# Three more units by rows, later output projections and earlier weight loads in an attention and gMLP kernel

## The chip, the cores and the metric

One core of one Trainium2 chip runs the whole program. The metric is the device time of one execution in microseconds (us), median of several runs. A ratio below is the mean time of one kernel's fast runs over the mean of the other's fast runs of the same rounds, so it is not quite the ratio of the medians quoted beside it. "Faster" or "slower" needs 2%. A *span* is the length of the one profiled execution, from its first to its last instruction, without the start and end of the launch.

## The reference, cut to what matters

```python
# S = 2048, D = 512, 32 query heads, 8 kv heads, Dh = 128, F/2 = 896
mod = (silu(c) @ w_mod).reshape(1, 6, 1, 512)
sa, ca, ga, sb, cb, gb = mod[:, 0], ..., mod[:, 5]
h = layernorm(x) * (1 + ca) + sa
q = (h @ wq) per head;  p = softmax(q @ k.T * Dh ** -0.5);  o = p @ v
x = x + ga * (o @ wo)
h = layernorm(x) * (1 + cb) + sb
z = gelu(h @ w_in);  z1, z2 = z[:896], layernorm(z[896:])
g = w_sp @ z2 + b_sp                      # spatial mixing, 2048 x 2048
out = x + gb * ((z1 * g) @ w_out)
```

## The kernel before

The attention is cut into NU = 128 *units*: 8 groups (one kv head with its 4 query heads) times 16 tiles of 128 queries (NT = 16; a *block* is CT = 4 tiles). *Iteration* u issues the scores of unit u in eight slots. In each slot TensorE also gets a share of an older unit's PV product and, mostly, one *extra*: a matmul of an output projection (`wo`) or of a query projection. A slot without an extra is *bare*. The *excess* of an iteration is its length less the sum of its matmuls at the pitches that the prediction measures.

An ordinary unit computes its scores transposed, so that ScalarE's exponentials can go straight into PV, one iteration later, as 64 matmuls of 129 columns. A unit *by rows* computes them untransposed; the exponentials are summed as they are made, VectorE normalises them, four DMA transposes of 512 KB turn them, and PV follows three iterations later as 16 matmuls of 512 columns.

Names in the profile lines: `hT` is the transposed layer norm, `oT` the transposed output of PV, `z` the hidden tile of the gMLP. The memory of a unit by rows is reused, so its rows stand there as `win_sb`, `wmod_a` or `pn`, and their transpose as `pT` or `wsp`.

```python
TURN_A, TURN_B = 2 * CT, NU - CT - 2          # units by rows: 8, 10, ... 120

def by_rows(u):
    return TURN_A <= u < TURN_B and u % 2 == 0
def pv_at(u):
    return u + 3 if by_rows(u) else u + 1
def wo_at(u):
    return pv_at(u) + (3 if TURN_A <= u < TURN_B else 2)
...
def turn_rows(u, hh):                          # VectorE, then a DMA transpose
    ...
    nc.vector.tensor_scalar(out=rows, in0=rows, scalar1=rinv, scalar2=None, op0=ALU.mult)
    nc.sync.dma_start_transpose(out=pTs[u][:, :, hh * P : (hh + 1) * P], in_=rows)
...
def mod_rows():                                # the rows ga and gb, on all partitions
    ...
    for i, (part, rows) in enumerate(((2, ga_rows), (5, gb_rows))):
        cols = slice(part * NDT, (part + 1) * NDT)
        nc.vector.tensor_copy(out=modc[:, cols], in_=mc_ps[:, i * NDT : (i + 1) * NDT])
        line = dram.tile([D], FP32, name=f"mod{part}")
        nc.gpsimd.dma_start(out=line[:].rearrange("(dt p) -> p dt", p=P), in_=modc[:, cols])
        nc.gpsimd.dma_start(out=rows[:], in_=line[:].partition_broadcast(P))
...
ln1_at(3, (5, 1), (5, 5), (7, 4))              # last layer-norm chunk: statistics, norm, turn
at(NU - CT - 1, 2, lambda: nc.gpsimd.dma_start(out=win_sb, in_=win_dram))
at(4, 4, mod_cols_b)
at(5, 4, mod_rows)

def set_fill(b):                               # query projection of block b as extras
    hole = TURN_A + 1 if (TURN_A + 1) // CT == b - 1 else None
    ...
    for k, fn in enumerate(fs):
        ...
        elif b == 2:
            it, slot = (5, k // 2) if k < 8 else (it, slot)
...
for g in range(1, HKV):                        # weights of group g
    it = (g - 1) * NT
    at(it + 9, 5, lambda g=g: load_k(g))
    at(*((5, 2) if g == 1 else (it + 7, 4)), lambda g=g: load_wq(g, nc.gpsimd))
    at(*((5, 2) if g == 1 else (it + 11, 4)), lambda g=g: load_v(g))
    at(*((5, 2) if g == 1 else (it + 13, 4)), lambda g=g: load_wo(g, nc.gpsimd))
```

`at(iteration, slot, f)` puts f's instructions at that place of every engine's order.

Of the kernel before, what the change touches and what calls it, by code (L numbers as in the profile page):

```python
# [11 lines left out]
FP32 = mybir.dt.float32  # L12
# [3 lines left out]
P = 128  # L16
# [559 lines left out]
def kernel(  # L576
# [19 lines left out]
    nc = tc.nc  # L596
# [3 lines left out]
    REP = HQ // HKV  # L600
# [9 lines left out]
    CT = 512 // P  # L610
# [17 lines left out]
    win_dram = B_w_in.rearrange("(dt p) f -> p dt f", p=P)  # L628
# [11 lines left out]
    stat = fast.enter_context(tc.tile_pool(name="stat", bufs=2))  # L640
# [10 lines left out]
    rall = res.tile([P, NT * HQ], FP32, name="rall")  # L651
# [5 lines left out]
    win_sb = win_t[:].rearrange("p (k f) -> p k f", k=NDT)  # L657
# [61 lines left out]
    def load_wq(g, engine):  # L719
        wqs[g] = early.tile([P, NDT, REP * DH], BF16, name="wq_g")  # L720
        engine.dma_start(
            out=wqs[g][:], in_=wq_dram[:, :, g * REP * DH : (g + 1) * REP * DH]
        )

    def load_v(g):
        v1 = late.tile([P, NKT, DV], BF16, name="v1")
        nc.gpsimd.memset(v1[:, :, DH:DV], 1.0)
        if g > 0:
            nc.gpsimd.dma_start(out=v1[:, :, 0:DH], in_=v_dram[:, g])
        else:  # L730
            nc.sync.dma_start(out=v1[:, 0 : NKT // 2, 0:DH], in_=v_rows)
            nc.sync.dma_start(
                out=v1[:, NKT // 2 : NKT, 0:DH], in_=v_dram[:, 0, NKT // 2 : NKT]
            )
        groups.setdefault(g, {})["v1"] = v1

    def load_wo(g, engine):
        wo_g = late.tile([P, REP, D], BF16, name="wo_g")
        engine.dma_start(out=wo_g[:], in_=wo_dram[:, g * REP : (g + 1) * REP, :])
        groups[g]["wo"] = wo_g  # L740

    def load_k(g):
        kT = early.tile([P, SK], BF16, name="kT")
        nc.sync.dma_start_transpose(out=kT[:], in_=A_k_cache[0, g])
        groups.setdefault(g, {})["kT"] = kT
# [154 lines left out]
    for k in range(2):  # L900
        for dt in (2 * k, 2 * k + 1):
# [3 lines left out]
            else:  # L905
                nc.scalar.activation(
                    out=dst,
                    in_=src,
# [17 lines left out]
    for hf, copy in enumerate((nc.vector.tensor_copy, nc.scalar.copy)):  # L926
        copy(
            out=qTs[0][:, 2 * hf : 2 * hf + 2, 0:P],
            in_=q_ps[hf][:, 0 : 2 * P].rearrange("p (h q) -> p h q", h=2),
# [3 lines left out]
    def qproj(b, heads, c0, n, banks=("misc", "misc")):  # L933

        g, ch = divmod(b, NCH)
        if b not in qTs:
            qTs[b] = early.tile([P, REP, 512], BF16, name="qT")
        one = n * len(heads) <= 512
        ps = {}

        def mm(hh, dt):
            if dt == 0 and (not one or hh == heads[0]):
                ps[0] = bank(banks[hh % 2])
            o0 = (hh - heads[0]) * n if one else 0
            nc.tensor.matmul(  # L945
                ps[0][:, o0 : o0 + n],
                lhsT=wqs[g][:, dt, hh * DH : (hh + 1) * DH],
                rhs=hTs[ch][:, dt, c0 : c0 + n],
                start=(dt == 0),
                stop=(dt == NDT - 1),  # L950
            )
            if dt == NDT - 1 and (not one or hh == heads[-1]):
                hs = heads if one else [hh]
                dst = qTs[b][:, hs[0] : hs[-1] + 1, c0 : c0 + n]
                src = ps[0][:, 0 : len(hs) * n].rearrange("p (h q) -> p h q", q=n)
                nc.vector.tensor_copy(out=dst, in_=src)  # L956

        return [lambda hh=hh, dt=dt: mm(hh, dt) for hh in heads for dt in range(NDT)]
# [4 lines left out]
    NU = HKV * NT  # L963


    TURN_A, TURN_B = 2 * CT, NU - CT - 2

    def by_rows(u):
        return TURN_A <= u < TURN_B and u % 2 == 0

    def pv_at(u):
        return u + 3 if by_rows(u) else u + 1

    def wo_at(u):
        return pv_at(u) + (3 if TURN_A <= u < TURN_B else 2)


    users, homes = dict(pT0=-2, pT1=-1, wsp=CT + 2), {}
# [8 lines left out]
    def at(it, slot, fn):  # L987
        later.setdefault((it, slot), []).append(fn)
# [198 lines left out]
    def load_wsp(tile_, t, st):  # L1187
        nc.sync.dma_start_transpose(
            out=tile_[:, st, :],
            in_=B_w_sp[t * 512 : (t + 1) * 512, st * P : (st + 1) * P],  # L1190
        )
# [35 lines left out]
    ln1_at(2, (2, 4), (3, 1), (4, 5))  # L1227
    ln1_at(3, (5, 1), (5, 5), (7, 4))
    at(2, 5, lambda: nc.gpsimd.dma_start(out=wmod_b, in_=wmod_dram[:, :, 2 * D : NMOD]))
    at(NU - CT - 1, 2, lambda: nc.gpsimd.dma_start(out=win_sb, in_=win_dram))  # L1230
    at(4, 4, mod_cols_b)
    at(5, 4, mod_rows)

    def set_fill(b):


        hole = TURN_A + 1 if (TURN_A + 1) // CT == b - 1 else None
        fs = qproj(b, list(range(REP)), 0, 512, ("misc", "o_ps" if hole else "misc"))
        for k, fn in enumerate(fs):
            it, slot = (b - 1) * CT + k // NDT, k % NDT  # L1240
            if hole:
                it, slot = divmod(hole * NSLOT + k // 2 - 1, NSLOT)
            if b == 1:
                it, slot = 2 + (10 + k) // 16, (5 + k // 2) % 8
            elif b == 2:
                it, slot = (5, k // 2) if k < 8 else (it, slot)
            fill.setdefault((it, slot), []).append(fn)

    def wsp0():
# [2 lines left out]
    at(NU + 1, 0, wsp0)  # L1252
    for st in range(NT):
        at(NU + 1 + st // 4, 2 * (st % 4), lambda st=st: load_wsp(wsp[0], 0, st))
    for g in range(1, HKV):
        it = (g - 1) * NT
        at(it + 9, 5, lambda g=g: load_k(g))
        at(*((5, 2) if g == 1 else (it + 7, 4)), lambda g=g: load_wq(g, nc.gpsimd))
        at(*((5, 2) if g == 1 else (it + 11, 4)), lambda g=g: load_v(g))
        at(*((5, 2) if g == 1 else (it + 13, 4)), lambda g=g: load_wo(g, nc.gpsimd))  # L1260


    zs = {}
# [90 lines left out]
    for it in range(NU + 6):  # L1354
        if it < NU:
            if it % CT == 0 and it // CT + 1 < NB:
                set_fill(it // CT + 1)
        elif it == NU:
            free_a.close()
            z2p = fast.enter_context(tc.tile_pool(name="z2p", bufs=1))  # L1360
            zs["z2"] = z2p.tile([P, NT, FH], BF16, name="z2")
        pvs = [u for u in (it - 5, it - 3, it - 1) if 0 <= u < NU and pv_at(u) == it]
        wos = [u for u in range(max(it - 6, 0), min(it - 2, NU)) if wo_at(u) == it]
        wf = [fn for u in wos for fn in wo_proj(u)]
        for i in range(NSLOT):
# [37 lines left out]
    for f in range(NFT):  # L1403
# [6 lines left out]
        out=ok1[:], in0=rall[:], scalar1=1.0 / SAFE, scalar2=None, op0=ALU.is_ge  # L1410
# [8 lines left out]
        out=bad[:], in0=okm[:], scalar1=-1.0, scalar2=1.0, op0=ALU.mult, op1=ALU.add  # L1419
# [137 lines left out]
```

## Time and profile before

| | before |
|---|---|
| time, three runs | 1315.22 us (1314.62 to 1316.67) |
| span of the profiled run | 1311.9 us |
| TensorE / ScalarE / VectorE busy | 99% / 85% / 52% |
| granted TensorE clock | 1.000 |
| period of two iterations in the steady part | 17.44 us |

The table says where not to look: the time is TensorE's, and it is a sum of equal periods. Only the head (iterations up to 13), the tail and 0.18 us per unit are left. The lines are in the prediction.

### The profile page before, as it was taken

How to read it: one execution, taken by the hardware profiler on the slowest of the kernel's cores; microseconds unless marked ns; L12 is line 12 of the kernel's file. 1: busy time of each engine (PE TensorE's matmuls, PEld its weight loads, DVE VectorE, ACT ScalarE, POOL GpSimd, SP SyncE). 2: the span in 40 equal slices, each digit the busy share in tenths (PEclk: the TensorE clock that was granted, in tenths of full speed). 3: DMA queues.
4: the chain of work that ended last, by engine and by line, in shares of the span. 5: the costliest groups of instructions: out<-in, count | busy, mean ns of one | idle time of the engine just before them, and what ended most of it. 6: DMA issues, size and time to landing. Idle time of an engine off the chain costs nothing.

```text
span 1311.9 us, 24470 instructions
## 1 busy us (share of the span) xinstructions
PE 1304.1 (99%) x9623; PEld 741.0 (56%) x9623; DVE 682.6 (52%) x1675; ACT 1111.1 (85%) x1517; POOL 54.0 (4%) x96
## 2 busy tenths in 40 slices
PE   9999999999999999999999999999999999999998
PEld 5665555555555555555555555555555556644445
DVE  5644544444445454444545444444454577884444
ACT  7899999999999999999999999999999998650000
POOL 1200000000000000000000000000000011120000
PEclk9999999999999999999999999999999999999999
DMA  7589778977787797779986798678866673254300
GB/s 181 119 118 178 130 140 147 148 130 149 153 156 142 140 140 142 142 139 136 160 162 121 144 142 156 124 150 153 153 125 128 116 131 85 58 138 100 73 20 27
DMA packets 592170, 170.51 MB, mean 130 GB/s; under 512 B 581712, under 2 KB 588112, under 8 KB 592048
## 3 DMA queue, kind: packets, MB, share of 16 engines
q1 hardware_dynamic: 585024, 149.74, 64.5%
q0 software_dynamic: 4432, 16.91, 5.1%
q10 hardware_dynamic: 2592, 2.23, 0.5%
q8 instruction: 77, 1.26, 0.4%
q14 instruction: 45, 0.37, 0.1%
HBM read 21.89 MB, written 2.10 MB: 18 GB/s over the span
## 4 chain that ended last, share of the span: by engine, by line
PE 98%; DMA 1%; DVE 0%; ACT 0%; SPq 0%; issue 0%; DVEq 0%
PE o_ps L1080 19%; PE s_ps L1024 18%; PE s_ps L1005 15%; PE o_ps L1059 15%; PE misc L1112 8%; PE misc L945 8%; PE misc L1437 7%; PE s_ps L1271 2%; PE s_ps L1310 2%; PE o_ps L1458 1%; DMA oT<-onorm 1%; PE o_ps L786 1%; PE s_ps L1458 1%; PE misc L855 0%; PE o_ps L945 0%; DVE hT L814 0%
## 5 line engine op out<-in xcount | busy, mean ns | idle before, releaser
L1031 ACT ACTIVATE pT<-s_ps 128x1024 bf16<-128x1024 f32 x560 | 568.5, 1024 | 34.4 <-PE s_ps L1024 11.3
L1080 PEld LDWEIGHTS <-pT 128*128 128x128 bf16 x4480 | 299.6, 98 | 130.8
L1080 PE MATMUL o_ps<-v,pT 128*128 128x129 bf16 x4480 | 344.6, 220 | 0.0
L1024 PE MATMUL s_ps<-qT,kT 128*128 128x512 bf16 x1136 | 337.6, 379 | 0.3 <-ACT pT L1031 0.2
L1005 PE MATMUL s_ps<-kT,qT 128*128 128x512 bf16 x912 | 271.2, 379 | 0.0
L1012 ACT ACTIVATE win_sb<-s_ps 128x1024 bf16<-128x1024 f32 x228 | 233.3, 1024 | 3.4
L1112 PE MATMUL misc<-wo_g,oT 128*128 128x512 bf16 x512 | 194.1, 379 | 0.7 <-DMA oT<-onorm 0.7
L945 PE MATMUL misc<-hT,wq_g 128*128 128x512 bf16 (+2 forms) x520 | 187.0, 371 | 0.1
L1024 PEld LDWEIGHTS <-kT 128*128 128x128 bf16 x1136 | 110.2, 98 | 114.6 <-issue 2.4
L1012 ACT ACTIVATE pn<-s_ps 128x1024 bf16<-128x1024 f32 x152 | 155.4, 1023 | 2.0 <-ACT wmod_a L1012 0.3
L1059 PEld LDWEIGHTS <-v 128*128 128x128 bf16 x912 | 89.2, 98 | 107.7
L956 DVE CAST qT<-misc 128x512 bf16<-128x512 f32 x125 | 85.6, 684 | 123.1 <-PE misc L945 123.1
L1068 DVE CAST oT<-o_ps 128x512 bf16<-128x512 f32 x57 | 39.4, 691 | 192.3 <-PE o_ps L1059 192.3
L1059 PE MATMUL o_ps<-wsp,v 128*128 128x512 bf16 x464 | 137.3, 379 | 0.0
L1059 PE MATMUL o_ps<-pT,v 128*128 128x512 bf16 x448 | 133.2, 379 | 0.0
L1005 PEld LDWEIGHTS <-qT 128*128 128x128 bf16 x912 | 89.1, 98 | 59.8 <-issue 0.2
L1045 DVE TENSOR_TENSOR tot<-rs 128x1 f32<-128x1 f32 x228 | 35.0, 153 | 127.7 <-ACT win_sb L1012 85.3
L1437 PE MATMUL misc<-wsp,z 128*128 128x512 bf16 (+2 forms) x560 | 100.7, 336 | 0.0
L1050 DVE TENSOR_SCALAR win_sb<-win_sb,rall 128x2048 bf16<-128x2048 bf16 x114 | 85.9, 753 | 4.2 <-DVE rall L1048 0.3
L1437 PEld LDWEIGHTS <-z 128*128 128x128 bf16 x560 | 50.6, 98 | 48.5
L1012 ACT ACTIVATE wmod_a<-s_ps 128x1024 bf16<-128x1024 f32 x76 | 77.8, 1024 | 0.0
L1125 DVE TENSOR_TENSOR xacc<-misc,xacc 128x512 f32<-128x512 f32 x112 | 76.1, 679 | 0.0
(110 smaller groups left out, 831.0 us busy)
## 6 DMA issues: line engine op xcount, KB each, us to landing
wq_g<-in_A_wq_dram POOLq DMA_DIRECT2D x7, 512.0 KB, 6.1
v<-in_A_v_cache_dram POOLq DMA_DIRECT2D x7, 512.0 KB, 6.3
wo_g<-in_A_wo_dram POOLq DMA_DIRECT2D x7, 512.0 KB, 10.6
wsp<-in_w_mod_dram POOLq DMA_DIRECT2D x1, 2048.0 KB, 10.8
out_dram<-yout ACTq DMA_DIRECT2D x16, 128.0 KB, 1.7
win_sb<-in_B_w_in_dram POOLq DMA_DIRECT2D x1, 1792.0 KB, 7.9
x_sb<-in_A_x_dram SPq DMA_DIRECT2D x3, 512.0 KB, 5.9
oT<-onorm SPq DMA_TRANSPOSE x71, 2.8
```

The lines of the kernel that those rows point to most:

```text
L945: nc.tensor.matmul(ps[0][:, o0 : o0 + n], lhsT=wqs[g][:, dt, hh * DH : (hh + 1) * DH], rhs=hTs[ch][:, dt, c0 : c0 + n], start=(dt == 0), s ...
L956: nc.vector.tensor_copy(out=dst, in_=src)
L1005: nc.tensor.matmul(s_ps[:, c * 512 : (c + 1) * 512], lhsT=qTs[b][:, hh, jj * P : (jj + 1) * P], rhs=groups[g]["kT"][:, k0 : k0 + 512], sta ...
L1012: nc.scalar.activation(out=rows_of(u, hh)[:, half * HK : (half + 1) * HK], in_=s_ps[:], func=ACT.Exp, scale=inv_sqrt_dh, accum_out=rsums[u ...
L1024: nc.tensor.matmul(s_ps[:, h * 512 : (h + 1) * 512].rearrange("p (r q) -> p r q", r=REP), lhsT=groups[g]["kT"][:, kt * P : (kt + 1) * P], ...
L1031: nc.scalar.activation(out=pTs[u][:, 2 * i : 2 * i + 2, :], in_=s_ps[:].rearrange("p (k q) -> p k q", k=2), func=ACT.Exp, scale=inv_sqrt_dh,)
L1050: nc.vector.tensor_scalar(out=rows, in0=rows, scalar1=rinv, scalar2=None, op0=ALU.mult)
L1059: nc.tensor.matmul(o_pss[u][:], lhsT=groups[g]["v1"][:, kt, 0:DH], rhs=pTs[u][:, kt, :], start=(kt == 0), stop=(kt == NKT - 1),)
L1080: nc.tensor.matmul(o_ps[:, hh % 2, 0 : DH + 1], lhsT=pTs[u][:, kt, hh * P : (hh + 1) * P], rhs=groups[g]["v1"][:, kt, 0 : DH + 1], start=( ...
L1112: nc.tensor.matmul(X_ps[:], lhsT=oTs[u][:, hh, :], rhs=groups[g]["wo"][:, hh, :], start=(hh == 0), stop=(hh == REP - 1),)
L1125: nc.vector.tensor_tensor(out=xaccs[j][:], in0=X_ps[:], in1=xaccs[j][:], op=ALU.add)
L1437: nc.tensor.matmul(g_ps[:, :n], lhsT=z2[:, st, f * P : (f + 1) * P], rhs=wsp[t][:, st, c0 : c0 + n], start=(st == 0), stop=(st == NT - 1 a ...
```

## The change

Its intent: give the cheaper PV to three more units, and fill or remove the small holes at the two ends of the attention.

```diff
-    TURN_A, TURN_B = 2 * CT, NU - CT - 2
+    TURN_A, TURN_B = CT + 2, NU - 2
...
     def wo_at(u):
-        return pv_at(u) + (3 if TURN_A <= u < TURN_B else 2)
+        return pv_at(u) + (3 if u < TURN_B - CT else 2)
...
-    at(NU - CT - 1, 2, lambda: nc.gpsimd.dma_start(out=win_sb, in_=win_dram))
+    at(NU - 2, 4, lambda: nc.gpsimd.dma_start(out=win_sb, in_=win_dram))
...
-            elif b == 2:
-                it, slot = (5, k // 2) if k < 8 else (it, slot)
...
+    def wait_for(u):
+        seen = stat.tile([P, 1], FP32, name="seen")
+        nc.gpsimd.tensor_copy(out=seen[:], in_=rall[:, u * REP : u * REP + 1])
+
+    at(5, 0, lambda: wait_for(3))
     for g in range(1, HKV):
         it = (g - 1) * NT
         at(it + 9, 5, lambda g=g: load_k(g))
-        at(*((5, 2) if g == 1 else (it + 7, 4)), lambda g=g: load_wq(g, nc.gpsimd))
+        at(*((5, 0) if g == 1 else (it + 7, 4)), lambda g=g: load_wq(g, nc.gpsimd))
         (load_v and load_wo likewise)
```

More of the change, by code (lines that the diff above doesn't have):

```diff
@@ L1257 @@
         at(it + 9, 5, lambda g=g: load_k(g))
-        at(*((5, 2) if g == 1 else (it + 7, 4)), lambda g=g: load_wq(g, nc.gpsimd))
-        at(*((5, 2) if g == 1 else (it + 11, 4)), lambda g=g: load_v(g))
-        at(*((5, 2) if g == 1 else (it + 13, 4)), lambda g=g: load_wo(g, nc.gpsimd))
+        at(*((5, 0) if g == 1 else (it + 7, 4)), lambda g=g: load_wq(g, nc.gpsimd))
+        at(*((5, 0) if g == 1 else (it + 11, 4)), lambda g=g: load_v(g))
+        at(*((5, 0) if g == 1 else (it + 13, 4)), lambda g=g: load_wo(g, nc.gpsimd))
     zs = {}
```

## The prediction

> **What bounds the kernel now.** I read the page's engine line first, then the chain of waits, then TensorE's timeline, and only then the DMA issues.
>
> ```profile
> PE 1304.1 (99%) x9623; PEld 741.0 (56%) x9623; DVE 682.6 (52%) x1675; ACT 1111.1 (85%) x1517; POOL 54.0 (4%) x96
> ...
> PE 98%; DMA 1%; DVE 0%; ACT 0%; SPq 0%; issue 0%; DVEq 0%
> ```
>
> TensorE holds 98% of the chain, and the only other share is one DMA wait of 1%. So nothing large can come from removing waits; a gain must be fewer or shorter TensorE pitches, or the few small holes. Since ends of matmuls are modelled, I take pitches from starts. Call the scores of unit u "iteration u"; it has eight slots, each with two score matmuls, a share of an older unit's PV, and perhaps one "extra" (an output-projection or query-projection matmul). Two neighbouring iterations of the steady part, from TensorE's timeline:
>
> ```profile
> 131.90 0.59 PE L1005 MATMUL s_ps<-kT,qT 128*128 128x512 bf16 x2
> 132.34 0.62 PE L1080 MATMUL o_ps<-v,pT 128*128 128x129 bf16 x8
> 132.79 0.38 PE L945 MATMUL misc<-hT,wq_g 128*128 128x512 bf16 x1
> 133.00 0.59 PE L1005 MATMUL s_ps<-kT,qT 128*128 128x512 bf16 x2
> ...
> 140.71 0.59 PE L1024 MATMUL s_ps<-qT,kT 128*128 128x512 bf16 x2
> 141.14 0.59 PE L1059 MATMUL o_ps<-wsp,v 128*128 128x512 bf16 x2
> 141.57 0.38 PE L945 MATMUL misc<-hT,wq_g 128*128 128x512 bf16 x1
> 141.79 0.59 PE L1024 MATMUL s_ps<-qT,kT 128*128 128x512 bf16 x2
> ...
> 149.34 0.59 PE L1005 MATMUL s_ps<-kT,qT 128*128 128x512 bf16 x2
> ```
>
> The first column is the start. An iteration that holds the PV of an ordinary unit (64 matmuls of 129 columns, L1080) takes 140.71 - 131.90 = 8.81 us; one with the PV of a unit by rows (16 of 512, L1059) 149.34 - 140.71 = 8.63 us. Eight small ones take about 0.454 us (0.0567 each), two wide ones 0.432 (0.216 each). A unit by rows is thus worth only 0.18 us of TensorE.
>
> Then I added, iteration by iteration, the matmuls at those pitches and compared with the distance of starts. From iteration 13 to 123 the difference is 0.01 to 0.02 us: TensorE never waits. It waits only in iterations 7 to 12 (0.90, 0.27, 0.15, 0.53, 0.37, 0.31, sum 2.53 us) and a little in 124 and 126 (0.19). Two kinds of wait:
>
> ```profile
> 79.63 0.39 PE L1112 MATMUL misc<-wo_g,oT 128*128 128x512 bf16 x1 [0.72 <-DMA oT<-onorm]
> ...
> 102.35 0.59 PE L1005 MATMUL s_ps<-kT,qT 128*128 128x512 bf16 x2
> 102.78 0.61 PE L1080 MATMUL o_ps<-v,pT 128*128 128x129 bf16 x8
> 103.35 0.59 PE L1005 MATMUL s_ps<-kT,qT 128*128 128x512 bf16 x2
> ```
>
> The first is an output projection that waits for its transposed input. The second is a slot with no extra: TensorE has 0.43 + 0.45 = 0.89 us of work, but the slot lasts 1.00, because ScalarE's exponential with its accumulator read repeats every 1.0 us in a unit by rows (100.19, 101.18, 102.18 in its timeline) and every 0.92 in an ordinary one. With an extra (1.10 us) TensorE is the slower. So bare slots cost, filled ones don't.
>
> Why the transpose was late stands in Pool's timeline and in the chain in order of time:
>
> ```profile
> 60.01 0.81 POOL L721 DMA_DIRECT2D wq_g<-in_A_wq_dram  x1
> ...
> 62.38 0.76 POOL L739 DMA_DIRECT2D wo_g<-in_A_wo_dram  x1
> ...
> 66.82 12.77 DMA oT<-onorm
> ```
>
> Group 1's three loads (512 KB each) were issued at 60 to 62 us, at the same moment as the four transposes of the last layer-norm chunk (61.0 to 66.7). Together they kept the DMA engines busy until about 76; this oT took 12.8 us where the median is 2.8.
>
> **What the Trainium skill says.** "TensorE: Matmul & The Clock Gate", Wait — 56ns, not 53.3ns?: start to start is N / 2.4 GHz + about 2.5 ns when warm; that gives 56.3 ns for 129 columns and 215.8 for 512. The trace agrees (56.7 and 216). The same page's Back-to-back issue gap says about 131 ns for a sustained stream at N = 512; here the measured 216 decides. "Perfetto Trace Analysis", Identifying the Most-Contended Engine, warns that matmul busy share is a poor measure; I therefore used starts, and they say the same. "DMA: Bandwidth & Descriptors", Issuing engines are not separate DMA queues: DMAs of different engines interleave on the same 16 engines. The 12.8 us landing beside Pool's loads agrees.
>
> **The change, part by part.** The order of instructions of the changed kernel, which I read slot by slot, has 144 matmuls fewer: 3 units x (64 - 16).
>
> Part 1, three more units by rows (6, 122, 124). TensorE: 3 x 0.18 = 0.54 us less, all on the path. ScalarE: 24 accumulator reads more, which count only in bare slots. VectorE: three more units at four times (0.15 + 0.16 + 0.75) + 0.69 = 4.9 us in place of 1.2: 11 us more, off the path.
>
> Part 2, the placement of extras. The first hole (an iteration without PV) moves from 9 to 7 and holds block 2's query projection instead of block 3's; block 2's eight early matmuls leave iteration 5; projections of units 0 to 7 come one later. Counting bare slots in the new order: iteration 8, 9, 11 and 12 are full in all slots, 6 and 10 keep four bare ones, 4 and 5 four bare ordinary ones, 7 is the old hole. I give each the excess that the same pattern had before: 6 as old 8 (0.27), 7 as old 9 (0.15), 10 as old 12 (0.31), 11 for its start 0.1, 4 and 5 0.05 each: 0.93.
>
> Part 3, the loads. Pool's copy reads the first reciprocal of unit 3, which comes halfway through iteration 4. That was 49.2 us; with four projections fewer ahead of it (4 x 0.216) about 48.3. So the loads start some 11 us earlier, into a stretch where the DMA engines had a busy share of 0.12 (54 to 60 us), and should be through before the transposes at about 60. Then no oT is late, also because projections get one more iteration; the 0.90 us in iteration 7 go. Taking 2.53 of before less the 0.93: 1.60 us saved at the head.
>
> Part 4, the tail. Iterations 124 (by rows) and 125 now have four bare slots each: about 0.3 and 0.15, less the 0.19 lost there before: 0.26 us lost. The double PV moves from 123 to 127, which costs nothing. The w_in load moves behind unit 124's rows; Pool reaches it at some 1110 us, 7.9 us to landing gives 1118, and the first use was at 1128.8: ten us to spare.
>
> Sum: 0.54 + 1.60 - 0.26 = 1.88 us. I take off 0.2 for the first rival below: 1315.2 - 1.7 = 1313.5 us, 0.13% less.
>
> **Rivals.** First, VectorE becomes the bound behind the attention:
>
> ```profile
> 1137.00:1145.00 8.00, 8.00 (x43) 4.10 (x42) 6.80 (x16) 4.18 (x5) 0.79 (x2) 1.00 0.45 83
> 1145.00:1153.00 8.00, 8.00 (x44) 4.08 (x42) 7.73 (x19) 4.16 (x6) 0.79 (x2) 1.00 0.42 92
> ...
> 1161.00:1170.00 9.00, 9.00 (x47) 4.41 (x46) 7.76 (x21) 5.36 (x6) 1.65 (x3) 1.00 0.55 116
> 1170.00:1184.00 14.00, 14.00 (x67) 6.38 (x66) 12.36 (x30) 8.37 (x9) 2.43 (x3) 1.00 0.46 103
> ```
>
> (The columns after the length are TensorE, weight loads, VectorE, ScalarE, Pool.) VectorE is nearly full here, and its last normalisation of z ends at 1182.7, while TensorE wants that tile about 2.6 us after 1183.1. The change moves one unit's output work (xacc, two products, statistics, norm, modulation: some 4.6 us) from iteration 125 to 129. VectorE's idle bits between 1134 and 1162 (1.65, 1.0, 1.95) take most of it, so its end slips by perhaps 1 to 2 us, while TensorE arrives 1.9 us earlier. For: the margin goes from about 3 to about 0. Against: it is still a margin. If it fails, 0.5 to 2 us are given back: 1314 to 1315.5.
>
> Second, the rows of unit 6 are late. Four 512 KB transposes now start at about 66 us; unit 8's last one was issued at 98.1, 15 us after its iteration began, and landed 6.9 us later, 2.8 us before its PV. Unit 6 has the same distance, with the layer-norm transposes ahead of it in the queue. If those delay it by 5 us, TensorE waits 2 us at iteration 9: 1315.5. Against it: the loads are out of the way.
>
> Third, the opposite: the holes at the head close more fully, because TensorE may run a slot ahead of ScalarE. That would give about 0.6 us more: 1312.8.
>
> **Range and chances.** The PV term is sure to 0.05 us, the head to some 0.6, the two rivals can each take up to 2 us, and the three runs of before span 2 us. 80% range: 1311.5 to 1315.7. Two per cent would be 26 us; the PV of three units is 0.5 and all the attention's holes together are 2.7, so faster by 2% cannot come from here. Slower needs a wait in each of many iterations, and the steady part is unchanged. Chances: 0.005, 0.99, 0.005.
>
> **What would show it.** L1059 x960 and L1080 x4352 with unchanged pitch; 9479 matmuls in all; no wait of L1112 for oT near 80 us; Pool's loads at 48 to 53 us and oT landings there of 3 to 5 us; iterations 6 to 12 with under 1 us of excess; four bare slots of about 1.0 us in iteration 124. I am wrong if TensorE waits for pT or wsp at iteration 9, if L1437's start is held by z (VectorE), or if the span moves by more than 4 us either way.

## More of the kernel before

`wsp` also holds the second half of `w_mod` until iteration 5.

`mod_rows` matters later: each of its rows goes to device memory and back (a *round trip*: a write of 2 KB whose elements lie 512 bytes apart on the device side of each partition, then a read of 256 KB onto all partitions), and Pool waits in its order for the first before it issues the second.

## The result, and the profile after

The changed kernel took 1314.13 us (1313.63 to 1314.46, 4 runs) against 1314.92 (1313.66 to 1316.67, 4 runs) for the kernel before in the same rounds: ratio 0.9993, 95% interval 0.9975 to 1.001, "same". The span fell from 1311.9 to 1311.8 us. So the predicted 1313.5 us was 0.6 off and inside the range, but the first profile showed 0.1 us saved where 1.88 had been summed up. The question was where the rest had gone.

The engine line and the shares of the chain, from the page of the changed kernel:

```profile
PE 1293.8 (99%) x9309; PEld 734.5 (56%) x9479; DVE 692.7 (53%) x1702; ACT 1113.5 (85%) x1541; POOL 55.5 (4%) x97
...
PE 97%; DMA 1%; issue 1%; DVE 0%; ACT 0%; SPq 0%; DVEq 0%
```

The counts are 9479 weight loads, 144 fewer than before, but only 9309 matmuls: 170 matmul records are missing from this trace. PE's busy time is therefore useless here (it seems to fall by 10 us). From here on I time TensorE by the starts of its weight loads, which are complete, and do so in all traces. VectorE grew by 10.1 us (11 predicted) and ScalarE by 2.4. The pitch is unchanged, as the weight loads of the first scores of three neighbouring iterations show:

```profile
122.49 0.31 PEld L1024 LDWEIGHTS <-kT 128*128 128x128 bf16 x2
...
131.12 0.31 PEld L1005 LDWEIGHTS <-qT 128*128 128x128 bf16 x2
...
139.93 0.31 PEld L1024 LDWEIGHTS <-kT 128*128 128x128 bf16 x2
```

8.63 us for the iteration with wide PV and 8.81 for the other: 0.18 us per unit, as before. Pool's timeline shows part 3 of the change, and also the two instructions that the prediction had passed over:

```profile
48.89 0.77 POOL L721 DMA_DIRECT2D wq_g<-in_A_wq_dram  x1
...
59.35 0.83 POOL L1184 DMA_DIRECT2D mod<-modc  x1
...
69.13 0.76 POOL L1184 DMA_DIRECT2D mod<-modc  x1
81.01 0.55 POOL L1185 DMA_DIRECT2D gb_rows<-mod  x1 [11.13 <-DMA mod<-modc]
```

The loads start at 48.9 us (predicted 48 to 53; 60.0 before), and the wait of the output projection for oT near 80 us is gone. But the two round trips of the modulation rows now stand alone in the stretch from 59 to 86 us, and the write of 2 KB is in flight for 8 to 12 us each time. In that stretch TensorE waited for the first shares of unit 6 (its timeline, then ScalarE's of iteration 6):

```profile
87.81 0.59 PE L1024 MATMUL s_ps<-qT,kT 128*128 128x512 bf16 x2
88.81 0.59 PE L1059 MATMUL o_ps<-pT,v 128*128 128x512 bf16 x2 [0.41 <-DMA pT<-wmod_a]
```

```profile
68.82 1.02 ACT L1012 ACTIVATE win_sb<-s_ps 128x1024 bf16<-128x1024 f32 x1 [0.77 <-PE s_ps L1005]
```

The first is rival 2 of the prediction: the weight loads show 0.87 us of waiting at iteration 9 where the undisturbed kernel has none. Not all of it is lost, since weight loads have some idle time anyway: iteration 9 has an excess of 0.56 us. The second is a late start of one exponential; with it iteration 6 has an excess of 0.85 us over its matmuls, where 0.27 was predicted.

At the tail I compare the last windows of the attention with those in the prediction (columns: length, TensorE, weight loads, VectorE, ScalarE, Pool, granted clock, DMA share, GB/s), and VectorE's last normalisation of z before and after:

```profile
1137.00:1145.00 8.00, 7.95 (x42) 4.07 (x42) 7.69 (x19) 3.89 (x5) 1.64 (x4) 1.00 0.45 84
...
1170.00:1184.00 14.00, 13.95 (x66) 6.39 (x66) 12.32 (x31) 8.37 (x9) 2.81 (x4) 1.00 0.46 103
```

```profile
1180.97 1.78 DVE L686 TENSOR_SCALAR z<-z,mvz,rstd_lnz 128x896 bf16<-128x896 bf16 x4 [1.47 <-POOL rstd_lnz L682]
```

```profile
1183.24 1.78 DVE L686 TENSOR_SCALAR z<-z,mvz,rstd_lnz 128x896 bf16<-128x896 bf16 x4 [1.47 <-POOL rstd_lnz L682]
```

(The first of the two lines is before, the second after.) VectorE took up the moved output work in its idle time after 1137 us (7.69 us busy instead of 6.80) and still ended 2.3 us later. TensorE did not wait for it in this trace.

The lead of the changed kernel over the trace of before, at the same instruction, adds it up. At the first score matmul it was -0.16 us (by chance; it varies from trace to trace). At iteration 14 it was +0.57, so the head gained 0.73 instead of 1.78 (1.60 for the holes and 0.18 for unit 6). At iteration 120 it was +0.09: three periods of the steady part were longer than 17.44 us, by 0.48 together. Unchanged by the tail but for +0.05, it was +0.14 at the start of the spatial stage, and 0.1 at the end. So 1.05 us were missing in the head and 0.48 in the steady part, and both had to be told apart: chance, or the change?

### The profile page after: what moved, and what is told of

It reads as the page before. It is cut to its first block, busy times and chain, and to the rows that moved or that the text cites. A ratio compares the mean times of both kernels' runs of the same rounds, so it can differ in the third digit from the quotient of the medians.

```text
span 1311.8 us, 24109 instructions
## 1 busy us (share of the span) xinstructions
PE 1293.8 (99%) x9309; PEld 734.5 (56%) x9479; DVE 692.7 (53%) x1702; ACT 1113.5 (85%) x1541; POOL 55.5 (4%) x97
## 4 chain that ended last, share of the span: by engine, by line
PE 97%; DMA 1%; issue 1%; DVE 0%; ACT 0%; SPq 0%; DVEq 0%
PE o_ps L1080 19%; PE s_ps L1024 18%; PE s_ps L1005 16%; PE o_ps L1059 15%; PE misc L1112 8%; PE misc L945 8%; PE misc L1441 7%; PE s_ps L1275 2%; PE s_ps L1314 2%; PE o_ps L1462 1%; PE s_ps L1462 0%; DMA wmod_a<-in_w_mod_dram 0%; DMA pT<-wmod_a 0%; PE misc L855 0%; PE o_ps L945 0%
## 5 line engine op out<-in xcount | busy, mean ns | idle before, releaser
L1031 ACT ACTIVATE pT<-s_ps 128x1024 bf16<-128x1024 f32 x544 | 552.8, 1024 | 29.4 <-PE s_ps L1024 7.9
L1080 PEld LDWEIGHTS <-pT 128*128 128x128 bf16 x4352 | 291.0, 98 | 127.0
L1080 PE MATMUL o_ps<-v,pT 128*128 128x129 bf16 x4352 | 334.8, 220 | 1.3
L1024 PE MATMUL s_ps<-qT,kT 128*128 128x512 bf16 x1088 | 323.4, 379 | 1.2 <-ACT pT L1031 0.2
L1005 PE MATMUL s_ps<-kT,qT 128*128 128x512 bf16 x935 | 280.1, 379 | 3.5 <-ACT win_sb L1012 0.4
L1012 ACT ACTIVATE win_sb<-s_ps 128x1024 bf16<-128x1024 f32 x240 | 245.4, 1023 | 5.0 <-PE s_ps L1005 0.8
L1112 PE MATMUL misc<-wo_g,oT 128*128 128x512 bf16 x470 | 178.1, 379 | 0.7
L945 PE MATMUL misc<-hT,wq_g 128*128 128x512 bf16 (+2 forms) x482 | 173.8, 370 | 0.8
L1024 PEld LDWEIGHTS <-kT 128*128 128x128 bf16 x1088 | 105.6, 98 | 114.0 <-issue 1.8
L1012 ACT ACTIVATE pn<-s_ps 128x1024 bf16<-128x1024 f32 x160 | 163.6, 1024 | 1.7
```

Of the source, the lines that this page charges most:

```text
L945: nc.tensor.matmul(ps[0][:, o0 : o0 + n], lhsT=wqs[g][:, dt, hh * DH : (hh + 1) * DH], rhs=hTs[ch][:, dt, c0 : c0 + n], start=(dt == 0), s ...
L1005: nc.tensor.matmul(s_ps[:, c * 512 : (c + 1) * 512], lhsT=qTs[b][:, hh, jj * P : (jj + 1) * P], rhs=groups[g]["kT"][:, k0 : k0 + 512], sta ...
L1012: nc.scalar.activation(out=rows_of(u, hh)[:, half * HK : (half + 1) * HK], in_=s_ps[:], func=ACT.Exp, scale=inv_sqrt_dh, accum_out=rsums[u ...
L1024: nc.tensor.matmul(s_ps[:, h * 512 : (h + 1) * 512].rearrange("p (r q) -> p r q", r=REP), lhsT=groups[g]["kT"][:, kt * P : (kt + 1) * P], ...
L1031: nc.scalar.activation(out=pTs[u][:, 2 * i : 2 * i + 2, :], in_=s_ps[:].rearrange("p (k q) -> p k q", k=2), func=ACT.Exp, scale=inv_sqrt_dh,)
L1080: nc.tensor.matmul(o_ps[:, hh % 2, 0 : DH + 1], lhsT=pTs[u][:, kt, hh * P : (hh + 1) * P], rhs=groups[g]["v1"][:, kt, 0 : DH + 1], start=( ...
```

## The experiments

By the 2% rule every kernel below is "same"; where one is called slower or faster in this section, it is by its 95% interval. Theory A: the sum in the prediction is right for an undisturbed head, and waits for DMAs at iterations 6 and 9, caused by the round trips, ate most of it. Rival B: the sum itself is wrong (the bare slots cost more, or the loads bring less). Rival C: the units by rows in the head make the waits, whatever else is on the queues. For the steady part: chance, or more DMA traffic.

Twelve kernels ran, two of them unchanged, in four sets, each set on one chip with the kernel before alongside. *Net head gain* is the lead over the first trace of before at iteration 14, less the lead at the first score matmul, which varied by some 0.7 us between traces (-0.17 to 0.55).

### The two kernels once more

No edit. For before again:

> The kernel before, unchanged, as a measure of chance: ratio to itself 1.000 with an interval of about 0.1%. In its trace the steady part (iterations 14 to 120) should again repeat every 17.44 us per pair without one odd period, and iteration 7 should again wait about 0.9 us for oT. If odd periods turn up here too, late transposes in the steady part are chance and belong to no version.

For after again:

> The changed kernel, unchanged. Its first trace lost 0.85 us in iteration 6 (0.27 expected), 0.57 in iteration 9 (a wait for the transposed rows of unit 6, 0 expected) and 0.48 in three odd periods of the steady part. Theory A (a property of the change: unit 6's transposes start into the slow round trips of the modulation rows): the wait at iteration 9 comes again, 0.4 to 1.5 us. Rival (chance): iterations 6 to 10 together lose under 1.1 us this time. Ratio to before 0.9990 to 0.9998.

Before again: 1315.62 us (ratio to before 1.0001, interval 0.9986 to 1.0017), span 1313.4. After again: 1312.72 (0.9983, 0.9969 to 0.9997), span 1310.8. The same program thus differs by 1.5 us between two spans. A line of TensorE's weight loads shows what an accident looks like, here in the kernel before:

```profile
264.39 0.13 PEld L1059 LDWEIGHTS <-v 128*128 128x128 bf16 x2 [1.19 <-issue]
```

This is a row unit's pT that landed late, in the steady part. Before again lost 1.03 us in that way, in two periods; after again 0.21 in one; the first trace of before none. So late transposes in the steady part belong to no version: that settles the 0.48 us as chance. In the head, after again had no wait at iteration 9 and no excess in 6, but lost 1.03 us at iteration 4, waiting for the second half of w_mod; its net gain was 0.76. By the expectation above this trace spoke for chance and against Theory A; what the round trips do is shown by the experiments that follow.

### Only the loads

```diff
+    at(5, 0, lambda: wait_for(3))
-        at(*((5, 2) if g == 1 else ...   # wq, v, wo of group 1
+        at(*((5, 0) if g == 1 else ...
```

> The kernel before with only the early loads (held by Pool's copy of unit 3's reciprocal). My prediction's step: loads issue at about 49 us, the oT wait of 0.9 us in iteration 7 goes, everything else stays; lead at iteration 14 0.9 us, time about 1314.3. Rival (the round trips of the modulation rows made that oT late, not the loads): the wait stays above 0.4 us.

1312.93 us (0.9984, 0.997 to 0.9997). Net head gain 0.87 us (0.9 expected); the wait it was to remove had been 0.90. Part 3 alone brings half of the head's gain.

### The changed kernel with the round trips moved into the steady part

```diff
     def mod_rows():
         ... (copies only)
+    def mod_spread():
+        ... (both rows: write of 2 KB, read of 256 KB)
+    at(22, 0, lambda: wait_for(20))
+    at(22, 0, mod_spread)
```

> The changed kernel with the two small round trips of the modulation rows (2 KB each, 8 to 11 us to landing) moved from iteration 5 to iteration 20. Theory A: the wait at iteration 9 goes, the transposes of unit 6 take about 3 us each in the queue instead of 5, iterations 6 to 12 lose 0.9 us as predicted, the lead over before at iteration 14 grows from 0.57 to about 1.3 us, time about 1313.2. Rival B (unit 6's transposes are late because the layer norm's four stand ahead of them in the queue): the wait at 9 stays within 0.2 us. Rival C: the round trips do the same harm wherever they lie, so a wait of 0.5 us or more turns up at iterations 21 to 25.

The net head gain was 1.88 us, with no wait at iteration 9; the excesses of iterations 3 to 12 were 0.16 (iteration 3), 0.26 (6), 0.14 (7) and 0.36 (10), sum 0.92 us. Predicted were 0.93. The three terms for 6, 7 and 10 came as predicted; the 0.16 in iteration 3 was not predicted (iteration 4 gave some 0.1 of it back), and the 0.2 predicted for 4, 5 and 11 did not come, so that the nearness of the two sums is partly luck. So rivals B and C of this section fall: unit 6 and its transposes are in the head here as well. (The expectation above letters its rivals differently: its B fell, its C came true, see below, and its time of 1313.2 us was missed by 12 us.) Two windows of 5 and 6 us in the head, first the changed kernel, then this one:

```profile
64.00:69.00 5.00, 4.95 (x52) 3.41 (x51) 2.70 (x8) 4.23 (x10) 0.43 (x1) 1.00 1.21 70
...
75.00:81.00 6.00, 6.00 (x41) 3.15 (x40) 3.31 (x8) 5.89 (x9) 0.00 (x0) 1.00 1.46 29
```

```profile
64.00:69.00 5.00, 5.00 (x54) 3.41 (x51) 2.70 (x8) 5.00 (x12) 0.00 (x0) 1.00 0.64 124
...
75.00:81.00 6.00, 6.00 (x41) 3.22 (x40) 2.73 (x6) 5.89 (x8) 0.00 (x0) 1.00 0.86 114
```

The last two columns tell it. With a 2 KB write in flight the DMA engines count as busier (1.21, 1.46; the share adds up the times of packets, which may overlap, so it can pass 1) and move less (70 and 29 GB/s). Without it they are less busy and move 124 and 114. The DMA issues of 58 to 92 us, in the same order, give the landing times that follow (last column, us):

```profile
hT<-xn SPq DMA_TRANSPOSE x4, 8.3
pT<-win_sb SPq DMA_TRANSPOSE x3, 12.7
```

```profile
hT<-xn SPq DMA_TRANSPOSE x4, 2.4
pT<-win_sb SPq DMA_TRANSPOSE x3, 4.9
```

As a whole the kernel took longer, 1325.20 us (1.0077, 1.006 to 1.0094): where the round trips now were, TensorE waited for a row unit twice, 3.08 us at iteration 23 and 3.84 at 25, and after each the granted clock was below 1 for some microseconds (0.50 in the 5 us behind the second). "TensorE: Matmul & The Clock Gate", What's actually happening, gives one idle window of about 3.4 us as what drops the clock to half, and as much sustained work to restore it. The second wait fits. The first was shorter than the figure (3.08 us by the weight loads, 2.62 in TensorE's timeline) and was followed by 0.82 and 0.84 in the 5 us windows, while a wait of 3.02 us in a later trace left 1.00. Here the measurement decides: a wait below the page's figure can lower the clock; no run shows what decided between these two. Together the two periods cost 11.2 us. My edit had a flaw, however: Pool takes its work in order, so the loads of group 2 queued up behind the round trips and came at 211 to 214 us instead of about 110. The second wait could have been theirs. The last experiment repairs this.

### The changed kernel with the loads where they were

```diff
-    at(5, 0, lambda: wait_for(3))
-        at(*((5, 0) if g == 1 else ...
+        at(*((5, 2) if g == 1 else ...
```

> The changed kernel with the loads of group 1 back at their old place (behind the layer norm of the last chunk, about 59 us) and without Pool's copy. If part 3 of the change is what makes room for unit 6 by rows: the layer norm's transposes again take 11 to 15 us to land, unit 6's four queue behind them, and TensorE waits 2 to 5 us at iteration 9; lead over before at iteration 14 from -2 to 0 us. Rival (the projections being one iteration later is enough, the loads do not matter): no wait above 0.5 us at iterations 8 and 9, lead 1.3 us or more.

1322.06 us (1.0051, 1.0035 to 1.0068). Two waits at iteration 9; the second, from TensorE's timeline:

```profile
94.81 1.01 PE L1059 MATMUL o_ps<-pT,v 128*128 128x512 bf16 x2 [3.64 <-DMA pT<-wmod_a]
```

With the 512 KB loads, the round trips and unit 6's transposes in one stretch the head loses 7 us (a lead of -2 to 0 us was expected, and a wait of 2 to 5). Part of it is the clock's: behind the first of the two waits, 3.35 us in TensorE's timeline, the granted clock was 0.63 and 0.69 in the windows of 90 to 95 and 95 to 100 us. Part 3 is thus more than its own 0.87 us: without it the rest of the change does harm.

### Only the head, only the tail

```diff
-    TURN_A, TURN_B = 2 * CT, NU - CT - 2
+    TURN_A, TURN_B = CT + 2, NU - CT - 2      # head only; with wo_at, fill and loads as in the change
+    TURN_A, TURN_B = 2 * CT, NU - 2           # tail only; with wo_at and the w_in load
```

> The change without its tail: unit 6 by rows, projections later, early loads; the last unit by rows stays 120. Against before, counted from each trace's own first score matmul: 1.7 us at iteration 14 if no chance wait falls into iterations 4 to 9 (0.9 from the loads, 0.18 from PV, 0.6 to 0.7 from fewer bare slots), and nothing after iteration 120. Time about 1313.

> The kernel before with only the tail: units 122 and 124 by rows and the later w_in load. Lead unchanged to iteration 120, then +0.1 us at the start of the spatial stage (0.36 from PV less 0.26 for bare slots), as three traces of the changed kernel show +0.05. Rival (VectorE or w_in late): TensorE waits before or at the start of the spatial stage, 0.5 to 2 us lost. Time within 0.1% of before.

Head only: 1313.47 us (0.9981, 0.9966 to 0.9996). Net head gain 1.89, nothing lost in the steady part, no wait at iteration 9, although the round trips are where the change has them. It is the third trace of that head: at iteration 9 one waited, two did not. Its last output tile was made 1.63 us ahead of before's, but the span is only 0.2 us shorter: from there to the end of the trace it had 5.3 us where before had 3.9. That final landing of an output is another chance of over a microsecond, and a reason to compare traces at an instruction and not by their spans.

Tail only: 1314.76 us (0.9992, 0.9977 to 1.0008). The lead grew by 0.05 us over the last iterations. Then the rival named first came true: TensorE's weight loads waited 0.51 and three times 0.33 us for z at the start of the spatial stage, and the last output tile came 0.81 us further behind before's than the spatial stage had started. VectorE had stood still for 3.72 us for the transposed norm of the last tile.

### Both rows in one round trip

```diff
+    at(4, 4, lambda: wait_for(3))             # and group 1's loads at (4, 4)
-    at(4, 4, mod_cols_b)
-    at(5, 4, mod_rows)
+    at(4, 7, mod_rows)                        # both writes
+    at(5, 4, mod_cols_b)
+    at(5, 4, mod_spread)                      # both reads
```

> The changed kernel with a shorter disturbance at the head: the loads of group 1 half an iteration earlier in program order, both modulation rows written out together at the end of iteration 4 instead of one after the other from iteration 5, read back in iteration 5, and the other modulation matmuls moved from iteration 4 to 5. If the serial round trips (59 to 86 us) are what delays unit 6's transposes, they are over by about 70 us: no wait at iterations 4 and 9, excess of iterations 2 to 12 about 0.9 us, net lead at iteration 14 1.7 to 1.9 us in this trace, time about 1312.5. Rival: two at once slow the layer norm's transposes and oT more, and a wait of 0.5 us or more turns up in iterations 6 to 9.

1312.44 us (0.9977, 0.9963 to 0.999), span 1310.3. The transposes of 58 to 92 us landed in 4.7 (hT) and 5.9 us (pT), there was no wait at iteration 9, and the net head gain was 1.53 (1.7 to 1.9 expected); iteration 6 had 0.59 us of excess from one late exponential. The edit changes three things at once (the loads, the writes, the place of the other modulation matmuls); the next kernel takes the round trips out altogether.

### The rows made on TensorE, without a DMA

```diff
+        mm: nc.tensor.matmul(ps, lhsT=sc_rep[:, kt, :], rhs=wmod_b[:, kt, row * D : (row + 1) * D])
+            # sc_rep: silu(c) repeated over 128 columns; 4 matmuls of 512 for each row, as extras
+        nc.vector.tensor_copy(out=rows[:], in_=ps)
```

(Also the step of the next experiment.)

> The changed kernel without the two round trips of the modulation rows: TensorE makes each row on all partitions with 4 matmuls of 512 columns (silu(c) repeated over 128 columns as weights), one in each of four bare slots of iterations 5 and 6. TensorE: 8 x 0.216 - 32 x 0.025 = 0.93 us more, less 0.25 us of bare slots filled in iteration 6; the norm of unit 127 is also moved as in the next kernel. If the round trips are what disturbs iterations 6 to 9: the hT and unit 6 transposes land in 2.4 to 5 us there (2.4 and 4.9 where the round trips were moved away, 8 and 12 with them), no wait at 6 to 9, net lead at iteration 14 1.88 - 0.7 = 1.2 us. Rival: waits of 0.3 us or more come in iterations 6 to 9 without the round trips too.

1312.46 us (0.9979, 0.9965 to 0.9993). hT and pT landed in 3.0 and 4.8 us, iterations 6 and 9 had neither excess nor wait. It pays eight matmuls of 0.216 us for 32 of 0.025 saved, 0.9 us, and in the profiled run, the slowest of its runs (1313.68), lost 0.81 us in iteration 4, waiting for w_mod: net head gain 0.34, where 1.2 was expected. It shows the cause without the cost of a better version.

### VectorE's last step behind two others

```diff
-        at(it + 2, 5, third)
+        at(*((it + 3, 1) if j == NT - 1 else (it + 2, 5)), third)
```

The modulation of the last tile, which waits for a DMA transpose, goes behind two statistics of z in VectorE's order.

> The changed kernel with one VectorE step moved: the modulation of the last unit (127) one iteration later, behind two statistics of z that do not wait. VectorE then does not stand 2 to 5 us before the transposed norm; the last four normalisations of z begin 1.5 to 2.5 us earlier against the start of the spatial stage (changed kernel: 0.65 and 1.36 us after it in its two traces; expected: 0.5 us or more before it). No wait of the spatial stage for z. Time as the changed kernel, since in its two traces TensorE did not wait there.

1314.33 us (0.9992, 0.9979 to 1.0006). The last normalisation of z started 1.40 us *before* TensorE's first spatial weight load, not 0.65 behind it as in the first trace of after. But this head was the worst of all four with the round trips in their place:

```profile
91.33 0.13 PEld L1059 LDWEIGHTS <-v 128*128 128x128 bf16 x2 [3.02 <-issue]
```

TensorE itself was thus 2 us late at the spatial stage, and most of the margin in this trace is that delay. Whether the step helps is left to the next trace. (The profiled run was also this kernel's slowest, 1315.76 us.)

### Both repairs together

```diff
+    (the edit of "Both rows in one round trip")
-        at(it + 2, 5, third)
+        at(*((it + 3, 1) if j == NT - 1 else (it + 2, 5)), third)
```

> Both repairs: the modulation rows written out together at the end of iteration 4 (as mod_pair) and unit 127's modulation later. As mod_pair, ratio to before 0.9975 to 0.9985, with no wait for z at the start of the spatial stage.

1312.59 us (0.9983, 0.9968 to 0.9998), span 1310.3; net head gain 1.86, no wait at iteration 9, z 1.28 us ahead of TensorE with TensorE on time.

### The round trips in the steady part, behind the loads

```diff
+    at(30, 0, lambda: wait_for(28))
+    at(30, 0, mod_spread)
```

> The changed kernel with both round trips of the modulation rows (scatter of 2 KB and broadcast read, twice in series) put behind unit 28's softmax, in the steady part, and behind the second group's loads in Pool's order; the earlier kernel with them behind unit 20 had delayed those loads by 100 us, so that it was open which of the two made TensorE wait. If the round trips alone hold up the row units' transposes: the second group's loads stand near 110 us as in the changed kernel, iterations 23 and 25 show no wait, and one or two odd iterations between 29 and 33 wait 2 to 4 us for pT, with the stretch of a scatter at under 60 GB/s; a slow clock behind a wait of over 3 us may add to it: 1316 to 1325 us. If the delayed loads had made the waits: no wait over 1 us anywhere in iterations 29 to 34, and about 1311.5 to 1313 us, for the head is undisturbed. In both cases no wait at iteration 9.

1318.50 us (1.0018, 1.0001 to 1.0035). Group 2's load of wq stood at 109 us again, iterations 23 and 25 did not wait (0.09 us in one period), and iteration 9 did not either. The first write was in flight from 256 to 265 us, the second from 267 to 280. Two windows, then the sync queue's transposes and TensorE's timeline:

```profile
260.00:265.00 5.00, 5.00 (x36) 2.64 (x34) 3.25 (x9) 4.94 (x8) 0.00 (x0) 1.00 1.59 31
...
275.00:280.00 5.00, 4.57 (x45) 2.89 (x43) 3.85 (x11) 4.96 (x11) 0.00 (x0) 1.00 1.75 23
```

```profile
274.26 16.07 SPq L1051 DMA_TRANSPOSE pT<-win_sb  x3
```

```profile
283.23 0.59 PE L1059 MATMUL o_ps<-wsp,v 128*128 128x512 bf16 x2 [3.67 <-DMA wsp<-pn]
```

In both windows the engines count as 1.6 to 1.75 busy and move 31 and 23 GB/s; the changed kernel moved 206 and 133 in the same ones. The transposes issued in the first write's flight landed after 9 to 14 us, just in time; those in the second's made iteration 31 wait 4.13 us by the weight loads, with the clock at 0.75 after it, and the period took 22.95 us instead of 17.44. So the round trips do it without group 2's loads. (Group 3's load of wq, next in Pool's order, slid to 280.8 us, but the wait had begun at 283.2 - 4.1 = 279.1.) In the earlier kernel the first wait, which began at 211.9 - 3.1 = 208.9 us, was likewise there before group 2's loads; how much of its second was theirs stays open.

### All heads together

| trace | round trips | hT, pT landing (us) | wait at iteration 9 | net head gain |
|---|---|---|---|---|
| after | in the head, in series | 8.3, 12.7 | 0.87 | 0.73 |
| after again | in the head, in series | 7.6, 11.4 | 0 | 0.76 |
| head only | in the head, in series | 7.9, 11.5 | 0 | 1.89 |
| after, last step later | in the head, in series | 9.5, 13.7 | 3.02 | -2.08 |
| both rows in one | earlier, in parallel | 4.7, 5.9 | 0 | 1.53 |
| both repairs | earlier, in parallel | 4.7, 5.8 | 0 | 1.86 |
| rows on TensorE | none | 3.0, 4.8 | 0 | 0.34 |
| moved to iteration 22 | none in the head | 2.4, 4.9 | 0 | 1.88 |
| moved to iteration 30 | none in the head | 2.4, 4.9 | 0 | 1.00 |

The landing times split cleanly: 7.6 us and more with serial round trips in the head, 4.7 and less for hT without. Whether TensorE then waits depends on the last microsecond: two of four did. (The head with the loads at their old place is left out; it had both disturbances.)

Two things that the table hides. First, a term of part 2 that I had overlooked: with the projections one iteration later, iteration 3 has four matmuls of 0.216 us fewer, so TensorE reaches the modulation matmuls of iteration 4 some 0.7 us earlier (48.3 us in after, 48.9 in before), and w_mod's second half, issued at about 37 to 38 us and landed 9 to 12 us later, can be too late for it. Before, then the kernel with the round trips at iteration 30:

```profile
48.92 0.91 PEld L855 LDWEIGHTS <-wsp 128*128 128x128 bf16 x32
```

```profile
48.69 0.86 PEld L855 LDWEIGHTS <-wsp 128*128 128x128 bf16 x32 [0.89 <-DMA wsp<-in_w_mod_dram]
```

Iteration 4 lost 1.03 us in after again, 0.81 with the rows on TensorE, 0.79 with the round trips at iteration 30 and 0.41 with the last step later. Of the four traces with iterations 3 and 4 as before, only before again lost anything there, 0.11. So this is mostly a cost of the change, and no effect of the round trips; no run took it out alone. Second, the gains are counted from the quickest of the three heads of the old kernel: with the same head, before again stands at -0.62 and tail only at -0.39, because iteration 7 lost 1.41 and 1.27 us there instead of 0.89.

## Why the prediction was right, and where its sum was off

**What held.** The time (1313.5 against 1314.13 and, in the second set, 1312.72) and the class. That says little of the mechanism: no gain at all, 1315.2, would have been in the range too. The PV term: 0.18 us per unit, with unchanged pitch. The loads: at 48.9 us, and 0.87 us gained alone against 0.90. The bookkeeping of bare slots, which had been the least certain step: 0.92 against 0.93 us, partly by luck as said above, and 1.88 and 1.89 of net head gain in undisturbed traces against 1.78. The tail: +0.05 us against 0.36 - 0.26 = +0.10, in every trace with that tail where it could be read.

**What failed.** It was the weight of the second rival. TensorE's wait for pT at iteration 9 was one of the prediction's own signs of being wrong, and it showed in after. Two of its signs of being right failed there as well: the excess of iterations 6 to 12 was 1.84 us instead of under 1 (0.67 in after again), and oT landed after 6.6 us instead of 3 to 5. "If those delay it by 5 us, TensorE waits 2 us at iteration 9 ... Against it: the loads are out of the way." I looked for what the change moved out of the stretch, and not for what remained in it. Two 2 KB writes remained, in the same Pool timeline that I had quoted from. They are among the smallest transfers of the kernel, and the DMA issues of before give them a median landing of 12.1 us, more than two of the three weight loads have there (4.2, 9.1 and 13.2). The runs showed that with them hT and pT land two to three times as late, and that two of four such heads then wait, by 0.87 and 3.02 us, which cost 0.56 and 2.72 us of excess. The mean of the four, (0.56 + 2.72) / 4 or about 0.8 us, is the size of the term for which I had put nothing (the 0.2 was for the first rival). The net head gain of the four averages 0.3 us instead of 1.78; the rest of the gap is the wait for w_mod in iteration 4, a mean of some 0.4, and the late exponential in iteration 6, some 0.3. With four single traces these means are rough. The "same distance as unit 8" argument was sound for a quiet queue: five traces without serial round trips in the head show no wait.

**The first rival.** VectorE's slip was given as 1 to 2 us and measured at 2.3. The margin "from about 3 to about 0" came true: no wait in after, 0.81 us lost in the tail alone. What I had not seen is that part of the slip is a wait, for the last tile's transposed norm: 1.95 us before, 2.15 in after, 3.72 and 5.24 in the two half changes. Moving that step gave the margin back.

**The third rival** (holes close more fully) did not occur: the excess was 0.92, not 0.3.

**What stays open.** The late exponential in iteration 6 (0.77 us in after, 0.92 in the trace with the later step, 0.59 with both rows in one round trip, there the last one of iteration 5) is absent in the seven others with the changed head, three of which have the round trips in place in series; no record shows what ScalarE waited for. In all three a 2 KB write was in flight just then (Pool issued the reads that wait for them at 68.6, 68.9 and 63.8 us), so the round trips are suspected, not shown. Nor is it shown how the 2 KB write slows its neighbours: the windows show that it does, and its length varied from 8 to 15 us. And the versions with a repaired or emptied head (1312.44, 1312.46 and 1312.59 us) lie below before's medians and below after's first, but level with after again (1312.72): the intervals of all four ratios overlap, so that none is shown to be the fastest.

## What to carry to other kernels

When a stretch is cleared of large transfers for the sake of a tight one, list what is *left* in it, by landing time and not by size. Where single profiles of one program differ by more than the gain in question, compare them at the same instruction and stage by stage, and give each wait a second and third trace before it is called an effect of the change. A change of parts should be judged with its parts taken out one by one: here one part was worth 0.87 us alone and 7 us in company.

## What the Trainium skill lacked or had wrong

- "DMA: Bandwidth & Descriptors", Rules for kernel authors, says that a strided last dimension lowers to one descriptor per element and should be made contiguous. It does not say what such a small write does to its neighbours. Here 2 KB took 8 to 15 us to land, the DMA engines moved 23 to 31 GB/s in 5 us windows beside it (206 and 133 without), and neighbouring 512 KB transposes landed in 11 to 16 us instead of 5. No run here counts the descriptors.
- "TensorE: Matmul & The Clock Gate", Back-to-back issue gap, puts a sustained stream at N = 512 at about 131 ns; all traces here have 216 ns, and 57 ns at 129 columns where the same place gives about 81 for 128. The formula that it calls isolated fits the stream.
- The same page, What's actually happening, has the clock drop after an idle window of about 3.4 us. Waits of 3.63, 3.84 and 4.13 us by the weight loads were followed by a lower granted clock, as it says; one of 3.08 us was too (0.82), one of 3.02 was not (1.00). In TensorE's timeline, where ends are modelled, these five are 3.35, 3.37, 3.67, 2.62 and 2.56 us.
- No page has the spread of a DMA transpose's landing. In the steady part of one and the same program a 512 KB transpose was late enough to hold TensorE by 0 to 1.0 us in a whole execution. Nor has any the spread of the last output's landing, which moved a span by 1.5 us.
